# Shift taps of the convolution's keys: from diagonal matmuls to VectorE products in 16 bits

## The chip, the cores and the metric

The kernel runs on one core of a Trainium2 chip. The metric is the device time of one execution in microseconds (us). Engines: TensorE (PE; PEld is its weight load), VectorE (DVE), ScalarE (ACT), GpSimd (POOL) and the queue engine SyncE (SP), which here only issues transfers.

## The reference

Two independent blocks are computed and laid side by side in the output, A in columns 0 to 511, B in columns 512 to 1023.

```
A: qkv = x @ wqkv;  32 heads of width 16, 2048 rows
   p = softmax(q k^T / 4);  out_A = (p v) @ wo
B: k_shift[s] = sum over m = 0..3 of k[s - m] * shift_k[:, m]     (rows before 0 are zero)
   kv = k_shift * v
   y  = causal convolution of kv with ssm_k along the 2048 rows (by channel, 512 channels) + kv * ssm_D
   out_B = q * y
```

All inputs and the output are bfloat16.

## The kernel before

The Python program is a planner: it keeps a modelled clock for each engine (the class `Eng`, L181 on), decides step by step which work goes where, and writes out one fixed order of instructions per engine with the semaphore waits they need. Nothing is decided on the chip. A step T (the loop at the end of the kernel function) emits one set of score matmuls, one exponential on ScalarE, then values matmuls and whatever side work fits in the planned gap.

**Attention.** There are 2048 score blocks of 128 keys by 512 queries (32 groups n, each four heads by 512 queries, times 16 key tiles, times the four heads, one on each row group of TensorE). `emit_qk` (L896 within `qk_mm`) makes scores in PSUM banks 0 to 4. ScalarE takes two or three blocks at once (`emit_exp`, L921). Some blocks go another way (`dve_block` decides): VectorE turns the scores into 16-bit integers (`exp_on_dve`, L1010), GpSimd makes from them, by integer additions on 64-bit words, three shifted copies (`shift_ready`, L1030), and the four copies times four scaled sets of values make up the exponential. So such a block needs four values matmuls, one from ScalarE only one (`emit_pv`, L1122). Such blocks use PSUM bank 7 (`BGB`) or 5 (`DB`). The constants at the top of the file (LOW, R_LIN, LIN_D, T_DVE and others) say how many may be under way.

**Side work** also uses bank 7 and TensorE: projections of queries, keys and values (`pe_unit` and `evac_unit`, kinds q, k, v), the output projection (op), the convolution (`conv_lags`, L1372, 32 small matmuls for each of 128 groups of four channels), its turn back (L1399), and, before the change, the kind kv. Side units have due steps in the lists `early` and `jobs`, worked out from PLAN and constants such as K0, KS, K1, C2 and C3. Where the plan leaves TensorE idle, `warm_up` puts in small matmuls that add zero (L1577).

**The shifted keys before.** The keys are first copied to a scratch in DRAM with the two halves of the rows interleaved (`kt_scratch`, LKR rows). Three transposing loads (`load_kt`) bring them to SBUF with channels on partitions (`KTR`). GpSimd writes diagonal 128 by 128 matrices of the taps (`make_dg`, L690). A unit kv (there are 16: four slabs c of 128 channels, four quarters i of the rows) multiplies transposed keys with the four diagonals, so that turning back, shifting, scaling and summing happen in one accumulation in PSUM, 16 matmuls a unit:

```
for m in range(4):
    c0 = LEFT + 2 * (64 * (4 * i + 3 - b) - m)
    ins = e.matmul(PS[:, bank, 128 * b:128 * b + 128], lhsT=KTR[kt_i][:, kt_c, c0:c0 + 128], rhs=DG[:, c, m, :],
                   start=(m == 0), stop=(m == 3))
```

VectorE multiplies the result with the values `VST` (loaded by `load_v`, L632) and writes `KV`; `spread_kv` copies half of KV to other partitions by a transfer. Slabs 0 and 1 are done before step 60 or so (K0, K1), slabs 2 and 3 in the ranges of steps C2 and C3. The convolution of channels in a slab waits for it, and so do the turned results of later attention groups (`may_turn`), since they lie in the place of the diagonals.

**The filter.** `ssm_k` is loaded as it is (`KZN`), VectorE writes it in reverse order (`kz_turn`, four copies of 2048 elements, L675), adds the skip factor `ssm_D` at lag zero (`kz_store`) and stores it to a second scratch, from which the convolution's operands `WR` are loaded, two rows for each group of channels (`feed_wr`), 256 transfers in all.

**VectorE's order.** Urgent results (PSUM banks that others wait for) are placed by `urgent`; other pieces stand in the streams of `flow`, and `advance` puts them in where VectorE is free. `todo` adds up what is still pending there, and `dve_block` admits a further block only while that is small.

**Queues.** SP issues nearly all transfers, in program order: an entry that waits holds what stands behind it, among them the queries of the next pair of heads (`QT<-QS`, eight transfers of 16 KB each time). GpSimd's queue carries the output and the convolution's q.

Of the kernel before, what the change touches and what calls it, by code (L numbers as in the profile page):

```python
# [14 lines left out]
S = 2048  # L15
# [34 lines left out]
KT_LATE = 2.5  # L50
E1 = 17
ES = 1
NE = 4
K0 = 36
KS = 3
K1 = 46
E2 = 80
V2 = (20, 30)
V3 = (16, 49)
C2 = (95, 160)  # L60
C3 = (215, 280)
LOW_2 = 2
LOW_L = 2
LEAD = 2
PRESS = 0
YIELD = -4
# [3 lines left out]
HURRY = 2  # L70
LOW = 6
# [19 lines left out]
MOST_OP = 2  # L91
OVER_OP = 0.1
R_ARR = 8
R_LIN = 6
LIN_D = 1.0
EVEN = 0.85
MOST_D = 3
MORE = 0.1
ALONE = 0.3
T_DVE = 6  # L100
SLOT = 4
OPEN = 40
CLOSE = 0
S_U = 0.6
S_FX = 0.55
S_T = 0.2
S_C = 0.2
PLAN = 600
PACE = 580
# [3 lines left out]
LOOK = 10  # L113
SAFE = -1
PRIOR = 1
HOT = 20
MIN_L = 0
MIN_A = 2
# [4 lines left out]
OP0 = 26  # L123
EVEN_MORE = 6
MOST_L = 3
MANY = 2
DELAY = 1
SOON_P = 0.2
RATE = 0.38
LAST_P = 2.0  # L130
TAIL_GAP = 2
AHEAD = 5
KZ_LATE = 8.0
# [11 lines left out]
NEAR = 0.1  # L145
FULL = 1.0
# [4 lines left out]
V512 = (0.60, 0.726)  # L151
SHIFT = {1: (0.4, 0.55), 2: (0.615, 0.765), 4: (1.05, 1.2)}
# [21 lines left out]
    (0, {"DELAY": 1, "EVEN_MORE": 6, "FIRST": 1, "HALF": 0.35, "HURRY": 2, "JOIN": 0.15, "JOIN_D": 0.7, "LAGS": 12, "LATE": 0.3, "LATE_D": 0.3, "LEAD": 2, "LIN_D": 1.0, "LOW": 6, "LOW_2": 2, "LOW_A": 5, "LOW_L": 2, "MARGIN": 0.25, "MARGIN_D": 0.1, "MARGIN_P": 0.1, "MIN_L": 0, "NOW": 4, "OPEN": 40, "OVER_C": 0.1, "PRESS": 0, "PRIOR": 1, "R_LIN": 6, "SAFE": -1, "SOON": 0.3, "SOON_P": 0.2, "S_FX": 0.55, "TURN": 0.2}),  # L174
# [131 lines left out]
def bass_concat_heads__mha_block__ssm_conv_h3__prompt_kernel(  # L306
# [25 lines left out]
    def sb(name, shape, dt=BF16):  # L332
# [26 lines left out]
    SHK = sb("SHK", [128, 4, 4])  # L359
# [8 lines left out]
    VST = [x.rearrange("p (t d) -> p t d", t=NB)  # L368
           for x in (WR[:, R_W - 2, 0:S], WR[:, R_W - 1, 0:S], OUTA[:, :, :].rearrange("p r d -> p (r d)"), OUTA[:, :, :].rearrange("p r d -> p (r d)"))]
    KZS = WRF[:, 0:4 * LKZ].rearrange("p (c m) -> p c m", c=4)  # L370
    DSS = WRF[:, 4 * LKZ:4 * LKZ + 4].rearrange("p (c m) -> p c m", m=1)
    KTR = [QNF[:, 0:2 * LKR].rearrange("p (c s) -> p c s", c=2),
           OTF[:, 4 * QB:4 * QB + LKR].rearrange("p (c s) -> p c s", c=1),
           OTF[:, 4 * QB + LKR:4 * QB + 2 * LKR].rearrange("p (c s) -> p c s", c=1)]
    KT_OF = [(0, 0), (0, 1), (1, 0), (2, 0)]
    DG = OTF[:, 12 * QB + 2 * LEFT:16 * QB + 2 * LEFT].rearrange("p (c m d) -> p c m d", c=4, m=4)
    KZN = [OTF[:, 4 * QB:4 * QB + 2 * S].rearrange("p (c s) -> p c s", c=2),
           QNF[:, 0:2 * S].rearrange("p (c s) -> p c s", c=2)]
    XN = RST[:, R_ARR - 1, 0, :, :]
    PS = enter(nc.psum_tensor("PS", [128, 8, 512], FP32))  # L380
# [84 lines left out]
    h_shk = dma(sp, d_tap, SHK[:, :, :], B_shift_k.rearrange("(c p) m -> p c m", p=128), kb=4)  # L465
# [7 lines left out]
    h_vn, h_kt = [], {}  # L473

    def load_v(c, dep=None):
        for x in range(2):
            src = bass.AP(tensor=v2.tensor, offset=v2[S // 2 * x + 64 * (NB - 1), 128 * c].offset, ap=[[D, 64], [-64 * D, NB], [1, 128]])
            h = dma(sp, d_kv[3 + c], VST[c][x:128:2, :, :], src, [dep] if x == 0 else (), kb=256)
        h_vn.append(h)
    for c in range(3):  # L480
        load_v(c)
# [9 lines left out]
    def load_kt(i, dep):  # L491
        c0, c1 = ((0, 256), (256, 384), (384, 512))[i]
        h_kt[i] = dma(sp, d_kv[i], KTR[i][:, :, :], kt_ap[:, c0:c1], [dep, h_kpair[0]], transpose=True, kb=(1024, 512, 512)[i])
        done[(id(h_kt[i][0]), h_kt[i][1])] += KT_LATE

# [39 lines left out]
    def unit_deps(u):  # L535
        if u[0] == "q":
            return h_x[PAIRS[u[1]][1]] + [h_wq[min(PAIRS[u[1]][0], 1)]]
        if u[0] == "k":
            return h_x[u[2]] + [h_wk[min(u[1], 1)]]
        if u[0] == "kv":  # L540
            return [h_kt[KT_OF[u[1]][0]], h_dg[0]]
        return h_x[u[2]] + [h_wv[min(u[1], 1)]]

    def ready(u):
        if u[0] == "q":
            return (u[1] < R_Q or 2 * (u[1] - R_Q) + 1 in qk_done) and (u[1] < 2 or 2 * u[1] - 1 in h_q and at(h_q[2 * u[1] - 1]) <= pe.t + 0.5)
        if u[0] == "k":
            return u[1] < 2 or LAST[u[1] - 2] in qk_done
        if u[0] == "v":
            return u[1] < 2 or LAST[u[1] - 2] in pv_done  # L550
        if u[0] == "op":
            return (PAIRS.index((3, u[1])) if u[1] < NQB - 1 else (15, u[2] + 1)) in h_otn and h_wop[0] is not None
        return KT_OF[u[1]][0] in h_kt and (u[1] < 3 or len(h_vn) > 3 and at(h_vn[3]) <= pe.t)

    def pe_unit(u, bank, parts=(0, 1, 2, 3)):
# [19 lines left out]
        elif kind == "kv":  # L575
            _, c, i = u
            kt_i, kt_c = KT_OF[c]
            deps += [h_kt[kt_i], h_dg[0]]
            mm_run = 0.239

            def mm(e, b):
                ins = None
                for m in range(4):
                    c0 = LEFT + 2 * (64 * (4 * i + 3 - b) - m)
                    ins = e.matmul(PS[:, bank, 128 * b:128 * b + 128], lhsT=KTR[kt_i][:, kt_c, c0:c0 + 128], rhs=DG[:, c, m, :],  # L585
                                   start=(m == 0), stop=(m == 3))
                return ins
# [19 lines left out]
    def evac_unit(u, bank, h):  # L607
# [18 lines left out]
        elif kind == "kv":  # L626
            _, c, i = u
            u0 = NB - 4 - 4 * i
            val = VST[c][:, u0:u0 + 4, :].rearrange("p b (q g) -> p b q g", g=4)
            src = PS[:, bank, :].rearrange("p (b q g) -> p b q g", b=4, g=4)  # L630
            dst = KV[:, 32 * c:32 * c + 32, u0:u0 + 4, :].rearrange("p q w g -> p w q g")
            hh = urgent(lambda e: e.tensor_tensor(dst, src, val, ALU.mult), [h, h_vn[c]], us=V512)  # L632
            if kv_n[c] == 3:
                spread_kv(c, hh)
            kv_n[c] += 1
            if sum(kv_n[0:2]) == 8 and c < 2:
                load_qn(0, [h])
                open_wr(2, hh, True)
            if c >= 2 and kv_n[c] == 4:
                h_kvm[c - 2] = h  # L640
            if c == 2 and kv_n[c] == 4:
                load_v(3, hh)
# [9 lines left out]
    kv_n = [0] * 4  # L652
# [9 lines left out]
    wr_late = []  # L662
    h_kzw = [None]
    h_kzt = [None]
    h_dg = [None]
    early_dve = []
    flow.append(early_dve)

    def piece(make, deps, us=V512, gate=lambda: True):
        early_dve.append(("k", deps, make, us, gate))  # L670

    def kz_turn(c, us):
        rev = KZN[c // 2][:, c % 2, :]
        rev = bass.AP(tensor=rev.tensor, offset=KZN[c // 2][:, c % 2, S - 1:S].offset, ap=[rev.ap[0], [-1, S]])
        h_kzt[0] = dve.op(lambda e: e.tensor_copy(KZS[:, c, 0:S], rev), [h_kzl], us=us)  # L675
        if c == 3:
            load_kt(0, h_kzt[0])

    def kz_store(us):
# [5 lines left out]
        load_kt(1, h_kzt[0])  # L685
        load_kt(2, h_kzt[0])
        open_wr(R_W - 2, h_kzw[0])

    def make_dg(us):
        h_dg[0] = pool.op(lambda e: e.affine_select(  # L690
            out=DG, in_=SHK[:, :, :].rearrange("p c (m i) -> p c m i", i=1).broadcast_to([128, 4, 4, 128]),
            compare_op=ALU.is_equal, fill=0.0, base=0, pattern=[[0, 4], [0, 4], [-1, 128]], channel_multiplier=1),
            [h_shk], us=(3.0, 3.1))

    piece(make_dg, lambda: [], (0.0, 0.0))
    for c in (2, 3, 0, 1):
        piece(lambda us, c=c: kz_turn(c, us), lambda: [h_kzl], gate=lambda: dve.t >= at(h_kzl) + KZ_LATE)
    piece(kz_store, lambda: [h_kzt[0]], (0.1, 0.22))
# [146 lines left out]
    def todo():  # L845
        return max(dve.t - pe.t, 0.0) + sum(us[0] for f in flow for _, _, _, us, _ in f)
# [99 lines left out]
    def ends():  # L946
        return max(max(dve.t, pe.t) + sum(us[0] for f in flow for _, _, _, us, _ in f) + V512[0], pool.t + PAIR * len(shifts)) + PAIR + LAST_P

# [260 lines left out]
    def finish_group(n, j, h):  # L1209
# [25 lines left out]
        def may_turn():  # L1235
            return 2 * p in h_mul and 2 * p + 1 in h_mul and (p < 4 or kv_n[2] == 4) and (p < 8 or kv_n[3] == 4)
# [75 lines left out]
    def open_wr(k, dep, staged=False):  # L1312
        if wr_rows[0] == R_W - 2 and not staged:
            wr_late.append((k, dep))
            return
# [5 lines left out]
        if staged:  # L1321
            for late in wr_late:
                open_wr(*late)
# [97 lines left out]
    early += [(K0 + KS * i, ("kv", 0, i)) for i in range(4)] + [(K1 + KS * i, ("kv", 1, i)) for i in range(4)]  # L1421
# [7 lines left out]
    jobs += [(a + (b - a) * i // 3, ("kv", c + 2, i)) for c, a, b in ((0, *C2), (1, *C3)) for i in range(4)]  # L1429
# [25 lines left out]
    def unit_step(T):  # L1455
        tight = False
        while not tight:
# [21 lines left out]
            us = pe.turn("F") + (0.445 if u[0] == "turn" else 0.478 if u[0] in ("kv", "v") else 2 * MM) + SWITCH  # L1479
# [243 lines left out]
```

## Time and profile before

| | before |
|---|---|
| median of three runs | 703.47 us (703.36 to 703.57) |
| the profiled execution | 703.51 us |
| its span in the trace | 701.8 us |
| busy, ScalarE / TensorE | 675.3 / 676.3 us |
| busy, VectorE / GpSimd | 541.8 / 515.7 us |
| score blocks on VectorE | 585 of 2048 |
| bytes moved by DMA | 164.25 MB, mean 234 GB/s |

How to read the lines that follow. A busy share is an average over stages; an engine that idles is only of interest if something waits for it. A group's row gives line, engine, operation, output and inputs with their shapes, the count, then busy us and mean ns of one, then idle time of the engine just before and who ended it. In a row of waits stand the one that waits and the one waited for, then total us, number of times and the longest. In a row of stretches stand the bounds, the length, then busy us with counts of PE, PEld, DVE, ACT and POOL, the granted clock as a share of full speed, the busy share of the DMA engines and GB/s. A line of the timeline gives start and duration in us.

### The profile page before, as it was taken

Reading aid. Unit: us, or ns where it says so; the run is one execution under the profiler, and the core shown is the slowest. Engines: PE = TensorE matmul, PEld = TensorE weight load, DVE = VectorE, ACT = ScalarE, POOL = GpSimd, SP = SyncE. Lnnn points to the kernel's source line nnn. Section 1 sums busy time; section 2 is a strip of 40 time slices with the busy share of each in tenths; the row PEclk is TensorE's granted clock in tenths of the full one; section 3 lists DMA queues with packets and bytes.
Section 4 is the critical chain, followed back from the end, with each engine's and each line's share of the span. In section 5 each row is a group of like instructions: output and inputs, shape, how many; then the busy total and the mean of one; then the engine's idle time right before and its main releaser. Section 6 shows DMA issues by size and latency. Waiting matters only on the chain.

```text
span 701.8 us, 26112 instructions
## 1 busy us (share of the span) xinstructions
PE 676.3 (96%) x11426; PEld 274.0 (39%) x11426; DVE 541.8 (77%) x880; ACT 675.3 (96%) x654; POOL 515.7 (73%) x638
## 2 busy tenths in 40 slices
PE   9999999999999999999999999999999999999998
PEld 4334334444334443433434434343333434234354
DVE  5788788887887778777887778878778687777873
ACT  6999999999999999999989999999999999999986
POOL 5566788777677667777768889778778777788871
PEclk9999999999999999999999999999999999999999
DMA  9998672478766469687876777788686876668311
GB/s 228 267 279 258 145 252 89 170 277 270 257 245 203 162 244 321 197 279 242 337 278 205 220 256 257 280 311 327 221 320 230 316 280 233 223 218 311 75 46 33
DMA packets 83047, 164.25 MB, mean 234 GB/s; under 512 B 41232, under 2 KB 47256, under 8 KB 82680
## 3 DMA queue, kind: packets, MB, share of 16 engines
q1 hardware_dynamic: 79720, 155.58, 65.6%
q0 software_dynamic: 2016, 6.69, 3.7%
q8 instruction: 91, 1.49, 0.8%
q10 hardware_dynamic: 1200, 0.33, 0.2%
q14 instruction: 20, 0.16, 0.1%
HBM read 149.17 MB, written 8.54 MB: 225 GB/s over the span
## 4 chain that ended last, share of the span: by engine, by line
ACT 46%; PE 41%; DVE 8%; POOL 3%; issue 1%
ACT PT L921 46%; PE PS L1122 16%; PE PS L896 13%; PE PS L1372 3%; DVE RST L1010 3%; PE PS L1287 2%; POOL RST L1030 2%; PE PS L564 2%; PE PS L585 1%; PE PS L573 1%; PE PS L596 1%; DVE DTN L1224 1%; DVE DT L1213 1%; PE PS L1399 1%; POOL out_dram L401 1%
## 5 line engine op out<-in xcount | busy, mean ns | idle before, releaser
L921 ACT ACTIVATE PT<-PS 128x1024 bf16<-128x1024 f32 (+1 forms) x648 | 672.3, 1192 | 17.1 <-PE PS L896 15.8
L1030 POOL INT64_ADD RST<-RST x600 | 489.1, 818 | 161.4 <-DVE RST L1010 122.1
L1010 DVE TENSOR_SCALAR RST<-PS 128x512 uint16<-128x512 f32 x585 | 396.1, 687 | 123.1 <-PE PS L896 118.3
L1122 PE MATMUL PS<-PT,VA 128*32 128x512 bf16 (+2 forms) x1618 | 273.4, 365 | 1.4 <-POOL RST L1030 1.3
L896 PE MATMUL PS<-QT,KTo 32*128 32x512 bf16 (+2 forms) x2248 | 258.1, 364 | 15.2 <-ACT PT L921 4.2
L1122 PE MATMUL PS<-RST,VS 128*32 128x512 bf16 (+1 forms) x1890 | 265.1, 369 | 1.6 <-issue 1.1
L896 PEld LDWEIGHTS PS<-QT,KTo 32*128 32x128 bf16 x2248 | 67.7, 91 | 188.4 <-ACT PT L921 107.3
L1122 PE MATMUL PS<-RST,VA 128*32 128x512 bf16 (+1 forms) x630 | 132.5, 370 | 0.7 <-DVE DT L1213 0.3
L1372 PE MATMUL PS<-WR,KV 128*30 128x128 bf16 (+7 forms) x4096 | 106.2, 220 | 0.7 <-DVE VA L647 0.7
L1122 PEld LDWEIGHTS PS<-PT,VA 128*32 128x32 bf16 x1618 | 66.7, 94 | 73.8 <-issue 46.1
L1372 PEld LDWEIGHTS PS<-WR,KV 128*32 128x32 bf16 (+7 forms) x4096 | 80.3, 101 | 32.7 <-issue 7.0
L1122 PEld LDWEIGHTS PS<-RST,VS 128*32 128x32 bf16 x1890 | 64.7, 95 | 55.4 <-issue 31.0
L1122 PEld LDWEIGHTS PS<-RST,VA 128*32 128x32 bf16 x630 | 33.4, 94 | 20.4 <-issue 10.6
L1213 DVE STREAM_TRANSPOSE DT<-PS 128x512 f32<-128x512 f32 x31 | 22.1, 713 | 3.0 <-PE PS L1122 2.2
L1388 DVE CAST YB<-PS 128x512 bf16<-128x512 f32 x32 | 21.7, 679 | 0.0
L1224 DVE TENSOR_TENSOR DTN<-DT,DR 128x256 bf16<-128x256 f32 x31 | 19.6, 634 | 0.8
L1287 PE MATMUL PS<-WKV,OTN 128*128 128x512 bf16 (+1 forms) x68 | 19.6, 372 | 0.4 <-DVE OTN L1262 0.3
L596 PE MATMUL PS<-WKV,xT 128*128 128x128 bf16 x256 | 18.6, 220 | 0.2
L573 PE MATMUL PS<-xT,WKV 128*128 128x512 bf16 (+1 forms) x64 | 17.0, 376 | 0.8 <-DVE QS L612 0.8
L1577 PE MATMUL PS<-IDN,ZW 128*32 128x128 bf16 (+3 forms) x78 | 17.1, 287 | 0.0
L596 PEld LDWEIGHTS PS<-WKV,xT 128*128 128x128 bf16 x256 | 14.4, 98 | 7.1 <-issue 2.3
L564 PE MATMUL PS<-xT,WQ 128*128 128x512 bf16 x60 | 16.6, 383 | 0.1
(73 smaller groups left out, 215.3 us busy)
## 6 DMA issues: line engine op xcount, KB each, us to landing
WR<-kz_scratch SPq DMA_DIRECT2D x256, 528.0 KB, 6.1
kz_scratch<-WR SPq DMA_DIRECT2D x4, 544.0 KB, 4.6
kt_scratch<-in_B_k_dram SPq DMA_DIRECT2D x1, 2048.0 KB
QN<-in_B_q_dram POOLq DMA_DIRECT2D x4, 512.0 KB, 8.5
out_dram<-QN POOLq DMA_DIRECT2D x4, 512.0 KB, 8.8
QT<-QS SPq DMA_DIRECT2D x120, 16.0 KB, 3.7
out_dram<-OUTA POOLq DMA_DIRECT2D x15, 128.0 KB, 3.5
QN<-in_B_ssm_k_dram SPq DMA_DIRECT2D x1, 1024.0 KB, 9.0
```

The costliest lines, as they stand in the source:

```text
L564: return e.matmul(PS[:, bank, :], lhsT=WQ[:, dc, o * 128:(o + 1) * 128], rhs=xT[:, dc, qb * 512:(qb + 1) * 512], start=(dc == 0), stop=(dc ...
L573: return e.matmul(PS[:, bank, c0:512], lhsT=WK[:, dc, o * 128:(o + 1) * 128], rhs=xT[:, dc, sc * 512 + c0:(sc + 1) * 512], start=(dc == 0) ...
L596: ins = e.matmul(PS[:, bank, 128 * j:128 * j + 128], lhsT=xT[:, dc, (4 * sc + j) * 128:(4 * sc + j + 1) * 128], rhs=WV[:, dc, o * 128:(o + ...
L896: ins = e.matmul(PS[:, bank, i * w:i * w + w], lhsT=KTo[32 * s:32 * s + 32, OF[n_] % 2, kt * 128:(kt + 1) * 128], rhs=QT[32 * s:32 * s + 3 ...
L921: h_exp[T] = act.op(lambda e: e.activation(PT[:, p0:p0 + n, :].rearrange("p b f -> p (b f)"), PS[:, banks[0]:banks[0] + n, :].rearrange("p ...
L1010: st["h"].append(urgent(lambda e: e.tensor_scalar(lin[:, 0, half, :].bitcast(U16), PS[:, bank, :], FIX_ADD, FIX_HI, ALU.add, ALU.min), [h, ...
L1030: return pool.op(lambda e: e.int64_add(dst, src, by * WORDS), deps, us=SHIFT[k])
L1122: ins = e.matmul(dst, lhsT=w, rhs=rhs, start=first, stop=last, tile_position=(0, 32 * s))
L1213: h_t = urgent(lambda e: e.transpose(out=dt, in_=PS[:, PVB, :]), [h, h_mul.get(n - 1)], slack=S_T, us=(0.63, 0.751))
L1224: h_mul[n] = dve.op(lambda e: e.tensor_tensor(dtn.rearrange("p (b i) -> p b i", i=32)[:, :, DH * r:DH * r + DH], blocks[:, :, 0:DH], rcp.b ...
L1287: ins = e.matmul(PS[:, b, c0:c1], lhsT=OTN[:, PAIRS.index((o, qb)), t * 128:(t + 1) * 128], rhs=WO[:, o, c0:c1], start=(o == 0), stop=(o = ...
L1372: ins = e.matmul(dst, lhsT=KV[:, channel(qd) // 4, 2 * n:2 * NB, g], rhs=WR[:, (2 * qd + g // 2) % (R_W), w0:w0 + 128], start=(n == 0), st ...
```

## The change

The kind kv is gone from TensorE, with the diagonals and the transposing loads. Instead the keys stay with rows on partitions. There are eight batches j of 256 channels by four row tiles. For each, `load_kv` loads the keys four times from the scratch, each time shifted by one row more (four transfers of 256 KB with runs of 512 bytes), and the values (two transfers). The taps are loaded to all partitions (`load_shk`, twice, in place of a load of 4 KB), and GpSimd spreads them into a free part of `KV` (`scales`). VectorE then runs eight instructions on 1024 elements a partition (`products`): four scalings in place, three additions, and the product with the values into `KV`. Each waits for the one before. Batches 0 and 1 are loaded at the start, 2 and 3 when the reversal copies have freed their place, 4 to 7 one after the other from a planned time LATE_KV on. The reversal of the filter (`kz_turn`) goes to GpSimd. The planner leaves the products out of what `todo` counts, except for a flat 2 us (BACK) while one of the first four batches is ready. Some forty of its constants have other values.

```
-KT_LATE = 2.5
-E1 = 17
+LATE_KV = 90
+GAP_KV = 10
+KV_RATE = 180
+BACK = 2
+E1 = 21
...
-LOW = 6
+LOW = 8
...
-R_LIN = 6
-LIN_D = 1.0
+R_LIN = 7
+LIN_D = 1.5
...
-T_DVE = 6
+T_DVE = 4
...
-PLAN = 600
-PACE = 580
+PLAN = 540
+PACE = 560
...
 V512 = (0.60, 0.726)
+V1024 = (0.75, 0.88)
+POOL_COPY = (2.4, 2.5)
+POOL_SCALES = (1.6, 1.7)
...
+    def load_kv(j, deps):
+        c0, u0 = 256 * (j // 4), 4 * (j % 4)
+        d = d_kv[min(j, 3)]
+        for m in range(4):
+            r0 = LEFT + 128 * (NB - 1 - u0) - 2 * m
+            src = bass.AP(tensor=kt_ap.tensor, offset=kt_ap[r0:r0 + 1, c0:c0 + 1].offset, ap=[[D, 128], [-128 * D, 4], [1, 256]])
+            dma(sp, d, KST[min(j, 3)][:, m, :, :], src, [*deps, h_kpair[0]] if m == 0 else (), kb=256, rate=KV_RATE)
+        for x in range(2):
+            src = bass.AP(tensor=v2.tensor, offset=v2[S // 2 * x + 64 * (NB - 1 - u0), c0:c0 + 1].offset, ap=[[D, 64], [-64 * D, 4], [1, 256]])
+            h = dma(sp, d, VST[j if j < 4 else j % 2][x:128:2, :, :], src, kb=128, rate=KV_RATE)
+        return h
...
-        h_kzt[0] = dve.op(lambda e: e.tensor_copy(KZS[:, c, 0:S], rev), [h_kzl], us=us)
-        if c == 3:
-            load_kt(0, h_kzt[0])
+        h_kzt[0] = pool.op(lambda e: e.tensor_copy(KZS[:, c, 0:S], rev), [h_kzl], us=POOL_COPY)
+        if c == 0:
+            h_kv[2] = load_kv(2, [h_kzt[0]])
+        if c == 1:
+            h_kv[3] = load_kv(3, [h_kzt[0]])
...
+    def scales(i):
+        def make(us):
+            h_ws[i] = pool.op(lambda e: e.tensor_copy(WS[:, i, :, :, :], SHK), [h_shk if i == 0 else h_shk2[0]], us=POOL_SCALES)
+            if i == 0:
+                h_shk2.append(load_shk(1, [h_ws[0]]))
+        piece(make, lambda: [], (0.0, 0.0), lambda: pe.t >= at(h_shk if i == 0 else h_shk2[0]), early_pool)
...
+    def products(j):
+        i = j // 4
+        k, v, u0 = KST[min(j, 3)], VST[j if j < 4 else j % 2], 4 * (j % 4)
+        last = [None]
+
+        def step(fn):
+            def make(us):
+                last[0] = dve.op(fn, [last[0] if last[0] is not None else h_kv[j], h_ws[i]], us=us)
+            piece(make, lambda: [last[0] if last[0] is not None else h_kv[j], h_ws[i]], V1024, gate=lambda: j in h_kv and h_ws[i] is not None)
+
+        def scale(m):
+            x = k[:, m, :, :].rearrange("p t (r e) -> p t r e", e=64)
+            w = bass.AP(tensor=KV.tensor if hasattr(KV, "tensor") else KV, offset=WS[:, i, m, 0:1, 0:1].offset,
+                        ap=[KV[:, 0, 0, :].ap[0], [0, 4], [8 * NB, 4], [1, 64]])
+            step(lambda e: e.tensor_tensor(x, x, w, ALU.mult))
+
+        def add(m):
+            a, b = [k[:, x, :, :].rearrange("p t d -> p (t d)") for x in (3, m)]
+            step(lambda e: e.tensor_tensor(a, a, b, ALU.add))
+        scale(3)
+        for m in (2, 1, 0):
+            scale(m)
+            add(m)
+        dst = KV[:, 64 * i:64 * i + 64, u0:u0 + 4, :]
+        a, b = [x.rearrange("p t (q g) -> p q t g", g=4) for x in (k[:, 3, :, :], v[:, :, :])]
...
     def todo():
-        return max(dve.t - pe.t, 0.0) + sum(us[0] for f in flow for _, _, _, us, _ in f)
+        wait = BACK if early_dve and kv_n[0] < 4 and early_dve[0][4]() and at(*early_dve[0][1]()) <= pe.t else 0.0
+        return wait + max(dve.t - pe.t, 0.0) + sum(us[0] for f in flow if f is not early_dve for _, _, _, us, _ in f)
...
-    early += [(K0 + KS * i, ("kv", 0, i)) for i in range(4)] + [(K1 + KS * i, ("kv", 1, i)) for i in range(4)]
...
-    jobs += [(a + (b - a) * i // 3, ("kv", c + 2, i)) for c, a, b in ((0, *C2), (1, *C3)) for i in range(4)]
```

More of the change, by code (lines that the diff above doesn't have):

```diff
@@ new lines, in bass_concat_heads__mha_block__ssm_conv_h3__prompt_kernel, with make @@
+    h_kv = {j: load_kv(j, ()) for j in range(2)}
+    h_row = []
+    def products(j):
[20 more added lines that the diff above has]
+        a, b = [x.rearrange("p t (q g) -> p q t g", g=4) for x in (k[:, 3, :, :], v[:, :, :])]
+        def make(us):
+            h = dve.op(lambda e: e.tensor_tensor(dst, a, b, ALU.mult), [last[0]], us=us)
+            kv_n[0] += 1
+            if j % 4 == 3:
+                for c in (2 * i, 2 * i + 1):
+                    spread_kv(c, h)
+                h_kvm[i] = h
+            if j < 2:
+                (open_row if h_kzw[0] is not None else h_row.append)(h)
+            if j == 2:
+                load_qn(0, [h])
+            if 3 <= j < 7:
+                piece(lambda us: later(j + 1, h), lambda: [], (0.0, 0.0), gate=lambda: pe.t >= LATE_KV + GAP_KV * (j - 3))
+            if j < 3:
+                products(j + 1)
+        piece(make, lambda: [last[0]], V1024)
@@ L946, in ends @@
     def ends():
-        return max(max(dve.t, pe.t) + sum(us[0] for f in flow for _, _, _, us, _ in f) + V512[0], pool.t + PAIR * len(shifts)) + PAIR + LAST_P
+        return max(max(dve.t, pe.t) + sum(us[0] for f in flow if f is not early_dve for _, _, _, us, _ in f) + V512[0], pool.t + PAIR * len(shifts)) + PAIR + LAST_P
     def dve_block(T, n_act, aside, chosen):
```

171 lines of the change are left out of this document (61 added, 110 removed).

## The prediction

> **What bounds the kernel now.** I read the page first: busy time by engine, then the chain that ended last.
>
> ```profile
> PE 676.3 (96%) x11426; PEld 274.0 (39%) x11426; DVE 541.8 (77%) x880; ACT 675.3 (96%) x654; POOL 515.7 (73%) x638
> ...
> ACT 46%; PE 41%; DVE 8%; POOL 3%; issue 1%
> ```
>
> Two engines are full at once, ScalarE (the exponentials) and TensorE, and the chain changes between them. Next the waits, longest first; the columns are total us, times, longest.
>
> ```profile
> POOL RST L1030 <- DVE RST L1010: 122.1, 146, 3.6
> DVE RST L1010 <- PE PS L896: 118.3, 317, 2.1
> PEld PS L896 <- ACT PT L921: 107.3, 274, 0.9
> ...
> PEld PS L1122 <- POOL RST L1030: 39.2, 154, 0.8
> ...
> ACT PT L921 <- PE PS L896: 15.8, 41, 1.6
> ```
>
> It is a ring. GpSimd waits for VectorE, VectorE for scores from TensorE, the score matmuls for a bank that ScalarE frees, and ScalarE hardly at all. So time falls only when ScalarE gets fewer of the 2048 score blocks, that is when VectorE and GpSimd take more of them by the shift road. The groups give the price of a block on each road, and a piece of the chain gives what values matmuls cost.
>
> ```profile
> L921 ACT ACTIVATE PT<-PS 128x1024 bf16<-128x1024 f32 (+1 forms) x648 | 672.3, 1192 | 17.1 <-PE PS L896 15.8
> L1030 POOL INT64_ADD RST<-RST x600 | 489.1, 818 | 161.4 <-DVE RST L1010 122.1
> L1010 DVE TENSOR_SCALAR RST<-PS 128x512 uint16<-128x512 f32 x585 | 396.1, 687 | 123.1 <-PE PS L896 118.3
> ...
> L1577 PE MATMUL PS<-IDN,ZW 128*32 128x128 bf16 (+3 forms) x78 | 17.1, 287 | 0.0
> ```
>
> ```profile
> 123.99 0.76 PE PS L1122 x12
> ```
>
> 585 blocks went to VectorE, so ScalarE had 1463: 672.3 / 1463 = 0.46 us each. A block on the other road costs VectorE 396.1 / 585 = 0.677 us and GpSimd 489.1 / 585 = 0.836 us, and it needs four values matmuls in place of one. Twelve of these took 0.76 us, so three more cost TensorE 0.19 us, and up to 0.25 us more (four matmuls) if its scores need a turn of their own.
>
> Last, three stretches of the run (length, then busy us of PE, PEld, DVE, ACT, POOL):
>
> ```profile
> 80.00:110.00 30.00, 29.00 (x430) 10.46 (x430) 25.53 (x41) 28.95 (x31) 23.03 (x29) 1.00 0.70 208
> 110.00:170.00 60.00, 59.23 (x1024) 24.72 (x1021) 48.48 (x77) 59.42 (x60) 45.87 (x56) 1.00 0.62 213
> ...
> 300.00:600.00 300.00, 291.17 (x5184) 114.80 (x5183) 237.29 (x373) 295.13 (x289) 233.01 (x286) 1.00 0.77 270
> ```
>
> VectorE held 79% over the long middle (237.29 / 300), 81% from 110 to 170 and 85% from 80 to 110 us. This is the share the forecast turns on.
>
> **The change, part by part.** What goes:
>
> ```profile
> sum 701.00, PE 18.63 PEld 14.35; mean PE 1.43 PEld 1.10
> ```
>
> ```profile
> L632 DVE TENSOR_TENSOR KV<-PS,WR 128x512 bf16<-128x512 f32 x8 | 5.5, 686 | 3.4 <-PE PS L585 3.4
> L632 DVE TENSOR_TENSOR KV<-PS,OUTA 128x512 bf16<-128x512 f32 x8 | 5.5, 684 | 0.9 <-PE PS L585 0.9
> ...
> L690 POOL TENSOR_SCALAR_AFFINE_SELECT OTN<-SHK 128x2048 bf16<-128x2048 bf16 x1 | 2.0, 2019 | 6.6 <-DMA SHK<-in_B_shift_k_dram 6.6
> ...
> L675 DVE COPY WR<-QN 128x2048 bf16<-128x2048 bf16 x2 | 1.5, 784 | 0.0
> ...
> L675 DVE COPY WR<-OTN 128x2048 bf16<-128x2048 bf16 x2 | 1.3, 632 | 0.0
> ```
>
> The first row is the sum of the stretches of line 585 alone, the diagonal matmuls: TensorE loses 18.6 us. VectorE loses the 16 products from PSUM (5.5 + 5.5) and the four reversals (1.5 + 1.3), 13.8 us. GpSimd loses the 2.0 us that made the diagonals. The bank of the side units also comes free 16 times.
>
> What comes: eight batches of eight VectorE instructions (four scalings, three additions, the product with the values), 64 in all, each with 1024 elements a partition, 16-bit, both inputs in SBUF. The trace has no such instruction. The nearest with two SBUF inputs are these (ns min/median/max):
>
> ```profile
> L1224 DVE TENSOR_TENSOR DTN<-DT,DR x31: 407/666/1079, 40.6 to 674.6; 128x256 bf16<-128x256 f32 x31
> ...
> L1257 DVE TENSOR_TENSOR DTN<-DT,DR x4: 224/445/765, 681.1 to 697.9; 128x64 bf16<-128x64 f32 x4
> ```
>
> ```profile
> L1224 DVE TENSOR_TENSOR DTN<-DT,DR 128x256 bf16<-128x256 f32 x31 | 19.6, 634 | 0.8
> ```
>
> Upper end: from 64 to 256 elements the shortest grew by 183 ns, 0.95 ns an element; 1024 would take 407 + 768 x 0.95 = 1.14 us, and with the mean excess of line 1224 over its shortest, 634 - 407 = 0.227 us, 1.37 us. Lower end: the 2048-element copy with one input took 0.632 us, half of it is 0.32 us. I take the 0.75 us that the diff writes down for this shape (V1024). It lies between, and its neighbour V512, 0.60 us, stands in the code against 0.677 us a block measured, so such figures are near what runs here. 64 x 0.75 = 48.0 us; net VectorE +34.2 us, to 576.0 us or 82.1% of the present span.
>
> GpSimd gets four reversals and two spreads of the taps. The nearest row is the 2.02 us of the diagonals (same 2048 elements); the code writes 2.4 and 1.6. I take the code's: 9.6 + 3.2 - 2.0 = +10.8 us, inside GpSimd's 161 us of idling. Bounds: 8 us (2.02 each for four) to 16 us (twice the row each). If that cover were gone it would delay shifts and so values matmuls, which now wait 39.2 us for GpSimd.
>
> The loads: keys come back from scratch four times (8 x 4 x 256 KB) in place of three transposes, and the taps as 2 x 256 KB.
>
> ```profile
> 0.00:60.00 60.00, 56.16 (x589) 22.67 (x589) 42.52 (x88) 53.31 (x50) 35.51 (x47) 1.00 0.98 259
> ```
>
> ```profile
> 14.58 10.51 SPq L401 DMA_DIRECT2D WR<-in_B_v_dram x4
> 25.12 2.08 SPq L401 DMA_DIRECT2D OUTA<-in_B_v_dram x2
> 27.25 4.54 SPq L401 DMA_DIRECT2D kt_scratch<-in_B_k_dram x2
> 31.83 0.65 SPq L401 DMA_DIRECT2D kt_scratch<-ZW x1
> 32.53 5.05 SPq L401 DMA_DIRECT2D QT<-QS x8
> ```
>
> The DMA engines are full for the first 60 us (share 0.98, 259 GB/s). Up to the first half of the products, before moved 2.0 (scratch) + 2.0 (transposes) + 1.5 MB (values), after moves 2.0 + 0.5 + 4 x 1.25 MB: 2 MB more, 8 us at that rate. On SP's queue the first two batches' 12 transfers wait for the scratch rows, and the QT<-QS of the second pair of heads stand behind them. I cost this at nothing, because the convolution is the only reader and its matmuls are spread over the whole run; the price if wrong is the 8 us. The third and fourth batches wait in SP's queue for GpSimd's reversals; behind them stand the filter rows, which need those reversals anyhow, and the later QT<-QS. Batches five to eight wait for the product before them, late enough that nothing but WR feeds stands behind.
>
> **The sum.** Were only TensorE and ScalarE to count, d blocks would move until both had gained the same: 18.6 - 0.19 d = 0.46 d gives d = 28.6 and 13.1 us (9.5 us at 0.44 us per block). That is the ceiling, 690.4 us. VectorE takes part of it: at a share s, 576.0 + 0.677 d = s (701.8 - 0.46 d). s = 0.84, a little under its best stretch: d = 12.7, a gain of 5.9 us. s = 0.821: nothing. s = 0.80: d = -14, 6.4 us lost. I choose 0.84 because the products may run whenever VectorE idles (they are not counted by the planner when it decides on further blocks) and 16 turns of the side bank are free. The profiled execution took 703.51 us around a span of 701.8, equal to the median 703.47 within 0.04, so 703.5 - 5.9 = 697.6, said as 698.
>
> **A rule that speaks against it.** Two instructions of line 1224 and GpSimd's beside them:
>
> ```profile
> 59.84 0.79 DVE L1224 TENSOR_TENSOR DTN<-DT,DR 128x256 bf16<-128x256 f32 x1
> ```
>
> ```profile
> 59.74 1.79 POOL L1030 INT64_ADD RST<-RST  x2 [0.26 <-DVE RST L1010]
> ```
>
> ```profile
> 40.60 0.41 DVE L1224 TENSOR_TENSOR DTN<-DT,DR 128x256 bf16<-128x256 f32 x1
> ```
>
> Started 0.10 us after a GpSimd pair, the product took 0.79 us; begun with GpSimd idle, 0.41. The Trainium skill, SBUF — State Buffer, section "SBUF: two separate sides", says that a VectorE instruction with two SBUF inputs and a GpSimd one that reads SBUF exclude each other for a whole instruction; the trace agrees with 0.79 against 0.41. The skill's VectorE: DVE Perf Modes, section on the perf-mode tiers, gives 1224 ns for a 2048-element 16-bit product, so an estimate of 0.69 us for ours, before such a wait; with it the sum would be 0.69 + 0.23 = 0.92 us each, near no change.
>
> **The rivals.**
> Lock: the 0.227 us comes on top of 0.75. 64 x 0.98 = 62.5 us, VectorE 590.5, at s = 0.84 d = -0.9: 703.9 us; at the upper end of 1.37 us, d = -25 and 715. Against it: 0.75 may hold the wait already. It decides from a mean of 0.97 us on.
> VectorE as the bound (the other side): VectorE cannot rise above some 80%, since it waits for scores in a fixed order; then d = -14 and 710 us; at today's 77%, 719. For it: 79% over 300 us with 118 us of waits that are not its own. It decides at a share of 82.1%.
> Early loads: the second pair's queries come late by the 8 us, ScalarE idles: 697.6 + 8 = 706 us. For it: share 0.98.
> Nothing: the freed TensorE time turns into more of line 1577's fillers (17.1 us now) and the count of blocks stays: 703.5 us. For it: fillers exist today, so TensorE's time is not short everywhere. Against it: it is full to 97% over the middle 300 us, and 16 turns of the side bank come free with it.
>
> **How the numbers follow.** Forecast 0.50; VectorE bound 0.17; lock 0.16, a quarter of it within 0.2%; early loads 0.08; nothing 0.05; others 0.04, spread on both sides. 0.2% (1.4 us) is about what a measurement can tell from no change. Faster 0.53, same 0.08, slower 0.39. The range leaves out the ceiling's last us and the far ends of the lock and of VectorE at 77%: 690 to 714. The forecast's own range is 690 to 702.
>
> **What would show it.** Line 585's group gone, 64 instructions near 0.75 us on VectorE; its share 83 to 85%; line 1010 at about 598 instead of 585 and ScalarE's busy time 6 us lower. Wrong if the count of line 1010 falls, if the new instructions take 1 us or more, or if ScalarE's waits in the first 80 us grow by several us.

## The result and the profile after

The changed kernel takes 714.81 us against 703.52 us: ratio 1.0162, 95% interval 1.0135 to 1.0188. The prediction was 698 us; the sign is wrong, and the time lies 0.8 us above the range's upper end. The profiled execution took 714.70 us around a span of 712.7 us, before 703.51 around 701.8, so 10.9 us of span are to be found. The page of the changed kernel, busy time and the chain that ended last:

```profile
PE 670.5 (94%) x11208; PEld 263.4 (37%) x11208; DVE 572.8 (80%) x922; ACT 679.4 (95%) x657; POOL 540.4 (76%) x645
...
ACT 41%; PE 32%; DVE 17%; POOL 6%; DMA 3%; issue 1%; SPq 1%
```

VectorE's part of the chain grew from 8 to 17%. The groups that answer to those shown before (line 949 is ScalarE's exponential, 1038 a block on VectorE, 1058 the shifts, 1597 the fillers):

```profile
L949 ACT ACTIVATE PT<-PS 128x1024 bf16<-128x1024 f32 (+1 forms) x651 | 676.5, 1172 | 24.5 <-PE PS L924 22.9
L1058 POOL INT64_ADD RST<-RST x602 | 505.4, 843 | 155.8 <-DVE RST L1038 121.0
L1038 DVE TENSOR_SCALAR RST<-PS 128x512 uint16<-128x512 f32 x583 | 391.0, 685 | 107.0 <-PE PS L924 101.8
...
L1597 PE MATMUL PS<-IDN,ZW 128*32 128x256 bf16 (+3 forms) x122 | 28.9, 290 | 0.8 <-DVE QS L600 0.4
```

VectorE took 583 blocks, not 598 (585 before). The 18.6 us of diagonal matmuls are gone, but TensorE's busy time fell by only 5.8: fillers rose from 17.1 to 28.9 us. Its waits for VectorE rose as well, before (first) and after (second):

```profile
PEld PS L896 <- DVE RST L1010: 24.9, 67, 1.1
...
PE PS L896 <- DVE RST L1010: 2.3, 9, 0.6
```

```profile
PEld PS L924 <- DVE RST L1038: 37.4, 84, 1.7
...
ACT PT L949 <- PE PS L924: 22.9, 53, 3.7
PE PS L924 <- DVE RST L1038: 10.5, 29, 1.2
...
PEld PS L1394 <- DMA WR<-kz_scratch: 3.9, 1, 3.9
PE PS L1394 <- DMA WR<-kz_scratch: 3.6, 1, 3.6
```

The tap instructions, by shape (the largest group, of 20, and the two extremes of the scalings):

```profile
L685 DVE TENSOR_TENSOR OTN<-OTN,KV 128x1024 bf16<-128x1024 bf16 x20 | 18.5, 923 | 0.0
...
L685 DVE TENSOR_TENSOR WR<-WR,KV 128x1024 bf16<-128x1024 bf16 x8 | 8.5, 1066 | 0.0
...
L685 DVE TENSOR_TENSOR QN<-QN,KV 128x1024 bf16<-128x1024 bf16 x4 | 2.9, 722 | 0.0
```

All 64 sum to 56.6 us, 0.885 each. Consecutive instructions overlap at their ends, so the added time on the engine is less: from the start of one to the start of the next, idle time left out, 0.82 us in the mean, 52.3 us in all, against the 0.75 that the planner used and the prediction took.

**Where the time went.** The trace gives the moment at which the N-th of the 2048 score blocks was finished (ends of lines 949 and 1038, counted):

| N | 100 | 200 | 300 | 600 | 700 | 1200 | 1300 | 2000 |
|---|---|---|---|---|---|---|---|---|
| before, us | 47.1 | 81.5 | 114.4 | 213.6 | 246.0 | 413.9 | 444.9 | 676.4 |
| after, us | 47.8 | 81.5 | 116.2 | 218.9 | 253.1 | 418.5 | 456.7 | 687.4 |
| lag, us | 0.7 | 0.0 | 1.8 | 5.3 | 7.1 | 4.6 | 11.8 | 11.0 |

There are two places. The first lies between 81 and 253 us (7 us, of which 2.5 are made up later), the second near 435 us (7 us at once). The stretches of both kernels, before first (the columns are those of the prediction: bounds, length, busy us of PE, PEld, DVE, ACT, POOL, granted clock, DMA share, GB/s):

```profile
42.00:95.00 53.00, 50.78 (x683) 20.09 (x678) 40.21 (x63) 50.76 (x48) 38.43 (x47) 1.00 0.82 225
95.00:240.00 145.00, 141.82 (x2373) 56.88 (x2370) 116.81 (x184) 143.40 (x143) 107.50 (x133) 1.00 0.62 211
```

```profile
42.00:95.00 53.00, 45.66 (x491) 14.87 (x495) 51.80 (x80) 51.12 (x45) 46.79 (x44) 1.00 0.66 211
95.00:240.00 145.00, 134.29 (x2131) 50.28 (x2123) 133.20 (x206) 140.23 (x136) 113.15 (x126) 1.00 0.69 219
...
430.00:435.00 5.00, 3.13 (x71) 1.28 (x67) 2.24 (x4) 4.03 (x4) 4.18 (x5) 1.00 1.02 257
435.00:440.00 5.00, 3.29 (x51) 0.94 (x51) 1.82 (x3) 2.27 (x3) 1.38 (x2) 0.75 1.03 420
440.00:445.00 5.00, 5.00 (x65) 1.60 (x64) 2.00 (x4) 3.10 (x4) 3.38 (x5) 0.56 1.02 414
445.00:450.00 5.00, 5.00 (x96) 1.95 (x93) 4.46 (x8) 5.00 (x7) 3.72 (x6) 1.00 0.64 202
```

From 42 to 95 us VectorE is busy for 51.80 of 53 us (98%; before 76%), from 95 to 240 us 92% (before 81%), and TensorE falls from 98 to 93% there. Near 435 us the granted clock falls to 0.75 and 0.56. TensorE's timeline after (start, length, then what was issued; the idle time before it in brackets) shows why:

```profile
436.71 0.65 PE L1394 MATMUL PS<-WR,KV 128*32 128x128 bf16 x32 [3.58 <-DMA WR<-kz_scratch]
437.29 0.83 PE L924 MATMUL PS<-QT,KTo 32*128 32x512 bf16 x6
```

A convolution step waited 3.58 us for its filter rows. SP's and GpSimd's timelines tell what held the rows:

```profile
412.64 9.63 SPq L401 DMA_DIRECT2D QT<-QS  x8
```

```profile
421.75 2.18 POOL L401 DMA_DIRECT2D QN<-in_B_q_dram  x2
```

SP's queue stood behind the queries of the next heads until 422.3 us, half a microsecond after GpSimd had begun to issue two loads of the convolution's q, 512 KB each. The view of the DMA issues (count, KB each, median us to landing), before from 395 to 420 us and after from 420 to 445 us:

```profile
WR<-kz_scratch SPq DMA_DIRECT2D x9, 528.0 KB, 5.1
QN<-in_B_q_dram POOLq DMA_DIRECT2D x2, 512.0 KB, 6.8
```

```profile
WR<-kz_scratch SPq DMA_DIRECT2D x11, 528.0 KB, 13.1
QN<-in_B_q_dram POOLq DMA_DIRECT2D x2, 512.0 KB, 10.6
```

Before, q was issued at 396.6 us and had landed by 405.2 us, and the next rows were issued from 402.7 us on, so the two hardly met. The wait, and the lower clock behind it, stand at the second loss; how much of it they make is for the runs below. The Trainium skill, TensorE: Matmul & The Clock Gate, Part 1, says that at least one idle window of about 3.4 us halves the clock, and that at least one busy window of that length brings it back; the trace agrees with 3.58 us of idling before the granted 0.75 and 0.56. If the clock was half, these two shares come to 2.5 and 4.4 us of it (an estimate), and it was back at 1.00 only about 8 us after work had begun again at 436.7 us.

### The profile page after: what moved, and what is told of

Read it like the earlier page. It is cut to its first block, busy times and chain, and to the rows that moved or that the text cites. A ratio compares the mean times of both kernels' runs of the same rounds, so it can differ in the third digit from the quotient of the medians.

```text
span 712.7 us, 25755 instructions
## 1 busy us (share of the span) xinstructions
PE 670.5 (94%) x11208; PEld 263.4 (37%) x11208; DVE 572.8 (80%) x922; ACT 679.4 (95%) x657; POOL 540.4 (76%) x645
## 4 chain that ended last, share of the span: by engine, by line
ACT 41%; PE 32%; DVE 17%; POOL 6%; DMA 3%; issue 1%; SPq 1%
ACT PT L949 41%; PE PS L1150 12%; PE PS L924 10%; DVE RST L1038 8%; POOL RST L1058 5%; PE PS L1394 3%; PE PS L1315 2%; DMA WR<-kz_scratch 2%; DVE OTN L685 2%; PE PS L574 1%; DVE OTN L689 1%; DVE DTN L1252 1%; PE PS L584 1%; PE PS L565 1%; DMA xT<-in_A_x_dram 1%
## 5 line engine op out<-in xcount | busy, mean ns | idle before, releaser
L1058 POOL INT64_ADD RST<-RST x602 | 505.4, 843 | 155.8 <-DVE RST L1038 121.0
L1038 DVE TENSOR_SCALAR RST<-PS 128x512 uint16<-128x512 f32 x583 | 391.0, 685 | 107.0 <-PE PS L924 101.8
L1150 PE MATMUL PS<-PT,VA 128*32 128x512 bf16 (+2 forms) x1620 | 279.4, 367 | 3.3 <-POOL RST L1058 2.8
L1150 PE MATMUL PS<-RST,VA 128*32 128x512 bf16 (+1 forms) x628 | 128.8, 371 | 2.2 <-POOL RST L1058 1.7
L1394 PE MATMUL PS<-WR,KV 128*32 128x128 bf16 (+7 forms) x4096 | 107.2, 221 | 3.6 <-DMA WR<-kz_scratch 3.6
L1150 PEld LDWEIGHTS PS<-PT,VA 128*32 128x32 bf16 x1620 | 69.8, 94 | 79.3 <-issue 49.2
L1394 PEld LDWEIGHTS PS<-WR,KV 128*24 128x24 bf16 (+7 forms) x4096 | 80.9, 101 | 36.7 <-issue 8.4
L1597 PE MATMUL PS<-IDN,ZW 128*32 128x256 bf16 (+3 forms) x122 | 28.9, 290 | 0.8 <-DVE QS L600 0.4
L685 DVE TENSOR_TENSOR OTN<-OTN,KV 128x1024 bf16<-128x1024 bf16 x20 | 18.5, 923 | 0.0
```

Source lines behind the costliest of these rows:

```text
L685: step(lambda e: e.tensor_tensor(x, x, w, ALU.mult))
L1038: st["h"].append(urgent(lambda e: e.tensor_scalar(lin[:, 0, half, :].bitcast(U16), PS[:, bank, :], FIX_ADD, FIX_HI, ALU.add, ALU.min), [h, ...
L1058: return pool.op(lambda e: e.int64_add(dst, src, by * WORDS), deps, us=SHIFT[k])
L1150: ins = e.matmul(dst, lhsT=w, rhs=rhs, start=first, stop=last, tile_position=(0, 32 * s))
L1394: ins = e.matmul(dst, lhsT=KV[:, channel(qd) // 4, 2 * n:2 * NB, g], rhs=WR[:, (2 * qd + g // 2) % (R_W), w0:w0 + 128], start=(n == 0), st ...
L1597: pe.op(lambda e, s=s, dst=dst, rhs=rhs, rows=rows, first=first: e.matmul(dst, lhsT=ZW[:, 0:rows], rhs=rhs, start=first, stop=first, tile_ ...
```

## The experiments

The first question was whether the first loss comes from the lock, GpSimd's adds being held up by tap instructions that read two tiles from SBUF (theory A), or is VectorE's own time (theory B); the letters are those of the expectations. For A speaks that adds that overlap a tap instruction took 1.07 us in the mean against 0.81 for the others, and that the chain of the changed kernel runs over GpSimd's adds and a GpSimd copy alone from 46.4 to 75.0 us; against it, block 200 comes at 81.5 us in both kernels. The second question was whether the filter row is the whole of the second loss.

**Taps replaced by fills, same order.**

```
-step(lambda e: e.tensor_tensor(x, x, w, ALU.mult))
+step(lambda e: e.memset(k[:, m, :, :].rearrange("p t d -> p (t d)")[:, 0:608], 1.0))
-step(lambda e: e.tensor_tensor(a, a, b, ALU.add))
+step(lambda e: e.memset(k[:, 3, :, :].rearrange("p t d -> p (t d)")[:, 0:608], 1.0))
```

> The 56 scalings and additions on VectorE are replaced by fills of 608 elements with a constant (near 0.68 us each, what the shortest scalings took, and no input in SBUF); the convolution's keys are thus not computed. The order of all instructions stays that of the changed kernel. Theory A (instructions with two SBUF inputs and GpSimd's additions shut each other out): GpSimd's 602 additions fall from 843 ns to about 815 ns, no GpSimd-bound stretch from 46 to 76 us, and some 7 us of the 10.9 us that the changed kernel lost go, about 708 us. Theory B (it is VectorE's time as such that is missing): the 64 instructions still take some 45 us, so at most 2 us are won, 713 us or more. Theory C (a late filter row at 433 us and the clock after it) is not touched: the wait of 3.6 us on that row and the lower clock are still there in both.

Measured: 707.97 us, ratio 1.0052 (1.0037 to 1.0068). The lag at block 700 is gone (246.3 us, before 246.0), and at block 1200 the kernel is 2.8 us ahead of before; then it loses the filter row's wait (5.2 us here). But the fill was shorter than the product that it was meant to equal:

```profile
L685 DVE MEMSET OTN<- 128x608 bf16 x20 | 11.3, 565 | 1.5
```

0.565 us, where a tap instruction without an add beside it takes 0.62 to 0.68. So it took away both causes at once, and A and B stayed apart no further than before.

**Taps kept with two SBUF inputs, but on 8 elements.**

```
-step(lambda e: e.tensor_tensor(x, x, w, ALU.mult))
+x8, w8 = k[:, m, 0, 0:8], WS[:, i, m, 0, 0:8]
+step(lambda e: e.tensor_tensor(x8, x8, w8, ALU.mult))
-step(lambda e: e.tensor_tensor(a, a, b, ALU.add))
+a8, b8 = a[:, 0:8], b[:, 0:8]
+step(lambda e: e.tensor_tensor(a8, a8, b8, ALU.add))
```

> The same 56 instructions keep their two SBUF inputs, their place and their waits, but work on 8 elements a partition in place of 1024 (the keys are not computed). Theory A: each still waits for a running GpSimd addition, but holds GpSimd up hardly at all; time near that of the fills, 707 us. Theory B: VectorE's busy time falls by some 40 us and now the loss goes, 707 us, while the fills stay at 713 us. So the two differ only in the fills, and this run says how much of the loss hangs on these instructions at all: if it stays above 712 us, neither A nor B is the cause.

Measured: 708.59 us, 1.0053 (1.0034 to 1.0073), block 700 at 245.9 us. Short instructions with the lock lose as little as short fills without it; again both A and B can say that (the lock is held for a shorter time).

**Second q load cut to 8 of 64 rows.**

```
-h_qn[i] = dma(pool, d_q[0], QN[64 * x:64 * x + 64, :, :], ...)
+n = 64 if i == 0 else 8
+h_qn[i] = dma(pool, d_q[0], QN[64 * x:64 * x + n, :, :], ...[0:n])
```

> The second load of q for the convolution's output (issued on GpSimd's queue at 421.8 us, 1 MB) moves 8 of each 64 rows, an eighth; the output of the second half of the convolution is not valid. Order unchanged. Theory C1 (this load delays the filter rows): the wait of 3.6 us at 433 us falls under 1 us, the clock stays at 1.00, about 709 us. Theory C2 (the rows were issued late, behind the transfers of the queries on SP's queue, and the DMA load does not matter): the wait stays near 3 us, 714 us.

Measured: 710.66 us, 1.0085 (1.0056 to 1.0113). The wait for the row is gone, and with it the drop of the clock, as the stretch from 430 to 450 us shows, after (first) and here (second):

```profile
430.00:450.00 20.00, 16.42 (x275) 5.77 (x272) 10.52 (x17) 14.39 (x16) 12.65 (x16) 0.83 0.93 323
```

```profile
430.00:450.00 20.00, 17.62 (x310) 6.57 (x307) 14.48 (x23) 17.86 (x19) 15.81 (x20) 1.00 0.86 316
```

The lag at block 700 stays (252.9 us). Between blocks 1200 and 1300 the lag now grows by 3.0 us in place of 7.1. So the meeting of q and the rows makes most of the second loss; what makes the other 3 us at this place stays open.

**Both: short fills and the small q load.**

> The fills of 608 elements in place of the 56 scalings and additions and the small second load of q together, order unchanged. If the two causes add up: e1 stood at 450.4 us at its 1300th block with a wait of 5.2 us on a filter row behind it; without that wait, and with the clock at 1.00, some 7 us less than e1, 700 to 702 us, which would account for the whole loss of the changed kernel. If the stall comes from the queue's order as well, or another wait takes its place, 705 us or more.

Measured: 704.00 us, 0.9999 (0.9972 to 1.0026), between the two expected ranges; block 700 at 245.7, block 2000 at 675.6 us. Against the kernel before of the same call the loss was 11.3 us in the changed kernel, 4.2 with the fills, 6.9 with the small q and 0.5 with both: the fills take away 7.1, the small load 4.4, the two 10.8. Within the two or three microseconds by which such differences are uncertain, the two causes add up to the whole loss.

**Both, with fills of 996 elements** (`[:, 0:608]` becomes `[:, 0:996]`, the small q load stays): a fill as long as the mean tap instruction, that reads nothing.

> As the run with fills and the small load of q together (ratio 0.9999 to before), but each of the 56 fills writes 996 elements in place of 608, so that it takes VectorE some 0.89 us, as long as the scalings and additions took with their waits (the keys are again not computed, the second half of q only in part). Theory A (what costs is that GpSimd is shut out): no change against the shorter fills, 702 to 705 us, GpSimd's additions near 814 ns. Theory B (VectorE's time itself): 18 us more on VectorE than with 608 elements bring the loss back, 708 to 711 us.

Measured: 714.94 us, 1.0140 (1.0113 to 1.0166), above even the 708 to 711 us expected for theory B. Adds, fills, and the waits of TensorE:

```profile
L1058 POOL INT64_ADD RST<-RST x602 | 488.0, 813 | 175.8 <-DVE RST L1038 140.2 <-DVE DR L1282 0.9 <-PE PS L1150 0.4
...
L685 DVE MEMSET OTN<- 128x996 bf16 x20 | 17.8, 888 | 3.1 <-DVE RST L1038 1.6 <-issue 1.3 <-DVE DTN L1252 0.2
```

```profile
PEld PS L924 <- DVE RST L1038: 39.0, 84, 1.8
PEld PS L1150 <- POOL RST L1058: 32.6, 128, 1.0
...
PE PS L924 <- DVE RST L1038: 15.1, 39, 1.3
```

GpSimd's adds are back at 813 ns (after: 843, before: 818) and its results are waited for less than before (32.6 against 39.2 us), yet the loss is there and larger, block 700 at 257.8 us, and TensorE's waits for VectorE are the changed kernel's and more. The run before it differs in the length of the fills alone and has its adds at 814 ns. That settles it for B: VectorE's time is enough to cost this much, with no add held up. It also gives a price. Added time on VectorE (start to start of all 64 instructions, plus the idle time before them) and loss, filter row out of the way:

| | added VectorE time, us | loss against before, us |
|---|---|---|
| short fills | 33.9 + 4.5 = 38.4 | 0.5 |
| the real taps | 52.3 | 6.9 |
| long fills | 51.8 + 9.0 = 60.8 | 10.7 |

A little under half a microsecond of time for each further microsecond of VectorE, from three points that are each uncertain by about 2 us, in an order written for shorter instructions.

The lock is not cleared by this, for it works on VectorE too. In the changed kernel 37 of the 64 tap instructions started while a GpSimd add was running. 35 of them ended 0.54 to 0.56 us after that add did, however long it still ran, and the 37 took 0.99 us in the mean; the other 27 took 0.68 in the median. That is about 37 x 0.31 = 11.5 us more on VectorE, and by the table's slope some 5 of the 6.9 us lost. This is an estimate: no run has full taps without the lock.

**The filter's reversal at half its length** (with the small q load; the copy moves 1024 32-bit words and doesn't reverse).

```
-h_kzt[0] = pool.op(lambda e: e.tensor_copy(KZS[:, c, 0:S], rev), [h_kzl], us=POOL_COPY)
+h_kzt[0] = pool.op(lambda e: e.tensor_copy(KZS[:, c, 0:S].bitcast(U32), KZN[c // 2][:, c % 2, :].bitcast(U32)), [h_kzl], us=POOL_COPY)
```

> As the run with the small second load of q (710.7 us), but the four filter copies on GpSimd move 1024 words of 32 bits in place of 2048 of 16 bits, and not in reverse order (the filter is thus wrong); order unchanged. If GpSimd's 8 us of reversals in the first 48 us are part of the loss, half of them gives 2 us or more back, 708.5 us or less; if the early stretch has cover, within 1 us of 710.7 us.

Measured: 710.44 us, 1.0075 (1.0052 to 1.0099), against 710.66 with the small q load alone. The copies took 1.03 to 1.14 us in place of 2.0 to 2.2. The reversal on GpSimd is hidden, to within the 1 us by which the lag at block 700 shrank (5.9 us, with the small q load alone 6.9).

**Q later by the plan**: `at(h_out[0]) < pe.t - 1.0` becomes `- 12.0`, with the order written anew from about 420 us on.

> The changed kernel whole, only the second load of q is issued some 8 us later by the plan (a margin of 12 in place of 1 us behind the first half's output); the plan changes from about 420 us on. Theory C1 (the load of q collides with the filter rows): no long wait on a filter row, clock 1.00, as with the small load, 707 to 711 us. If the collision only moves, one wait of over 2 us on a filter row elsewhere and 713 us or more.

Measured: 713.20 us, 1.0122 (1.0084 to 1.0160). The wait for the filter row shrank to 1.0 us and the clock stayed at 1.00, but VectorE now waited 3.1 us for q, and the lag grew from 6.8 us at block 1300 to 8.6 at block 2000. Moving the load moved the wait.

**TensorE's relief alone**: the kernel before with one diagonal matmul in place of four, and the plan told so.

```
-mm_run = 0.239
+mm_run = 0.06
-for m in range(4):
+for m in range(1):
-us = pe.turn("F") + (0.445 if u[0] == "turn" else 0.478 if u[0] in ("kv", "v") else 2 * MM) + SWITCH
+us = pe.turn("F") + (0.445 if u[0] == "turn" else 0.12 if u[0] == "kv" else 0.478 if u[0] == "v" else 2 * MM) + SWITCH
```

> The kernel before with one diagonal matmul in place of four in each kv unit (three of four taps are left out, so the convolution's keys are not the reference's); the planner is told that such a unit is short, all constants stay. TensorE so loses three quarters of the 18.6 us, and VectorE and GpSimd pay nothing. Theory D (my sum: freed TensorE time turns into blocks for VectorE): 18.6 x 0.75 = 14 us freed, three quarters of the ceiling of 13.1 us, some 694 us and 20 blocks more on VectorE. Theory E (the count of blocks is set by banks, queues and the planner's conditions, and freed time ends in fillers): count within 5 of 585, 701 to 705 us.

Measured: 701.03 us, 0.9958 (0.9930 to 0.9986).

```profile
L1010 DVE TENSOR_SCALAR RST<-PS 128x512 uint16<-128x512 f32 x585 | 393.9, 687 | 120.4 <-PE PS L896 116.1
...
L1577 PE MATMUL PS<-IDN,ZW 128*32 128x512 bf16 (+3 forms) x82 | 19.9, 288 | 0.6 <-DVE DT L1213 0.6
```

Three quarters of the diagonal matmuls gone for nothing in return bring 2.4 us and not one block more. **The same with the constants chosen anew** (some 40 of them, LOW_A, JOIN_D, K0, PACE and the like):

> The kernel with one of four taps on TensorE (three taps left out) and constants chosen anew for it; its order puts 598 blocks on VectorE. Theory D with a fitting order: 13 blocks x 0.46 = 6 us of ScalarE less than before, 694 to 698 us. Theory E holds in the strict form (freed TensorE time is worth nothing) if it is above 700 us.

Measured: 701.73 us, 0.9971 (0.9952 to 0.9991). Now VectorE has 598 blocks, and the gain is no larger: ScalarE waits 17.8 us for scores (12.4 without the new constants) and TensorE 3.4 us for filter rows. At block 1000 this order is 3.4 us ahead of before and at block 1200, with the longest of these waits between, 1.1; what it would gain without them is open.

**Is it the constants that came with the change?** The changed kernel with the constants that both kernels have (28 of them, PLAN, PACE, T_DVE, R_LIN and others) put back to the values before:

> The changed kernel with the 28 constants that both have set back to the values of before; the products, the loads and the reversal on GpSimd stay. The order puts 579 blocks on VectorE (585 before, 583 changed). Theory A (lock) and E (count of blocks): 6 blocks fewer cost ScalarE 6 x 0.46 = 2.8 us and the lock some 7 us, 711 to 714 us without a stall. If the loss of the changed kernel came from its other constants, this one is below 707 us.

Measured: 716.94 us, 1.0175 (1.0133 to 1.0217), above the 711 to 714 us expected. Putting them back does not bring the time back. This order loses in part elsewhere: it lags 5.9 us at block 700, 8.3 at block 2000 and 13.6 at the last.

**A plan that knows of the longer instruction**: 0.60 us for a tap instruction, 0.25 more and 0.5 on GpSimd's clock where GpSimd is busy, and constants chosen for it.

```
-V1024 = (0.75, 0.88)
+V1024 = (0.60, 0.73)
+held = pool.t > dve.t
+last[0] = dve.op(fn, ..., us=(us[0] + 0.25, us[1] + 0.25) if held else us)
+if held:
+    pool.t += 0.5
```

> The changed kernel with a planner that knows of the exclusion: a product that finds GpSimd busy is planned 0.25 us longer, and GpSimd 0.5 us later; its constants are chosen anew for that. 578 blocks on VectorE. Theory A: the cost of the lock stays (GpSimd's additions near 840 ns) but no longer pushes TensorE's order out of step, so some 4 to 8 us of the 10.9 us come back, 703 to 708 us. If 712 us or more, foresight does not help.

Measured: 709.22 us, 1.0059 (1.0033 to 1.0085), 5.3 us over before in place of 11.3 and just above the 703 to 708 expected. It has no wait for a filter row, and the lag at block 700 is 9.2 us, larger than in the changed kernel; at block 1200 it is 5.1 and at block 2000 4.9 us. What it gains on the changed kernel it gains at the second place; foresight of the length did not mend the first loss.

None of the runs of the full computation beats the kernel before. Whether another placing of the taps could is open. Holding SP's order alone fixed, and full taps without the lock, were not tried.

## Why the prediction was wrong

**The step that failed is the choice of the share in the sum, s = 0.84 and with it d = +12.7.** The blocks went to d = -2 and VectorE's share to 80.4% (572.8 / 712.7). Of the reasons given for 0.84, that the products may run whenever VectorE idles is the one the traces refute: the products land between 42 and 240 us, where VectorE was at 76 and 81% and went to 98 and 92%. An average over 700 us hid how little idle time there was where the work came: 41 us (198 less 40.2 and 116.8), of which the change used 28, and the score blocks no longer got their turn in time. The equation had a second fault: it gave all time to ScalarE's blocks. With the measured share of 0.804 it gives d = -11, and -2 was measured. ScalarE has two blocks more and its idle time grew from 26.5 to 33.3 us, because scores came late behind VectorE.

**TensorE's 18.6 us** were sized rightly and the diagonals are gone, but they bought nothing: 11.8 us became fillers, and the waits for VectorE rose by 12.5 us at the weight loads and 8.2 at the matmuls. The ceiling of 13.1 us falls as well. With three quarters of the relief for free the chip gave 2.4 us, and 13 more blocks gave no more. That the ring turns TensorE's time into blocks at 0.46 us each was argued from waits and did not show in either run.

**The price of a tap instruction**, 0.75 us: 0.885 us as the trace has it, 0.82 from start to start, so 52.3 us in place of 48.0. Without an add or a copy running on GpSimd as it starts it takes 0.62 to 0.68 us, with an add 0.92 in the median. The estimate of 0.69 + 0.23 = 0.92 us in the prediction, from the Trainium skill's VectorE: DVE Perf Modes, section on the perf-mode tiers, came nearest to the mean. Put into the prediction's own formula, 52.3 us would have moved the point of no change to a share of 82.7% and the gain from 5.9 to 4.0 us, so by that formula this term explains 1.9 of the 17 us by which the forecast is off.

**The rivals.** VectorE as the bound is the nearest: 710 us at s = 0.80, against 710.7 with the filter row taken out. Its mechanism held, by the stretches and the long fills; its sum did not, since it had d = -14 where the count hardly moved and the time was lost in waits, so that the two numbers agree is luck. Its chance of 0.17 was too small: the row that spoke for it, 79% over 300 us with waits that were not its own, was quoted, and the choice went by the best stretch instead. The lock is real (0.2 us on each instruction in the mean) and stayed below the 0.97 us from which it decides by the prediction (0.96 by its own formula). But that mark prices VectorE's time in blocks alone; at the price measured in the runs with fills, the lock is by estimate some 5 us of the loss. Early loads: block 200 comes at 81.5 us in both kernels; the extra 2 MB were hidden, as costed. Nothing: its mechanism, more fillers and the same count, came true, its time not.

**GpSimd** was right: the reversals and spreads took 10.9 us where 12.8 was costed, and half the reversal's time changes 0.2 us by the medians.

**What no step named** is the second place, 4.4 us of the time by the run with the small q load. The prediction followed SP's queue at the start, and not what a new order does to a load of 1 MB on GpSimd's queue 400 us later.

## What to carry to other kernels

Where the order is written out beforehand, work moved to another engine has to fit the idle time of the stretch where it lands; look up the share there, not over the run. Time freed on one engine of a ring is worth what the next engine can take, and a run that frees it for nothing tells that before anything is built. An instruction that has to wait out one of a neighbour engine costs its own engine that wait: here 0.99 us in place of 0.68. After a new order, look for the one transfer that now meets another: a single wait of 3.6 us, with the lower clock behind it, cost 4.4 us.

## What was not expected of the hardware

A VectorE fill of 608 16-bit elements took 565 ns and of 996 elements 888 ns, 0.83 ns an element, with about 0.16 us of idle time before each long one (9.0 us before 56), where the tap products had none. A 16-bit product of 1024 elements from SBUF, 0.62 us at its shortest, took up to 2.26 us: that one began at 42.82 us beside a reversing copy on GpSimd and ended 0.54 us after the copy, as those begun beside an add did. A GpSimd copy of 2048 16-bit elements in reverse took 2.0 to 2.2 us. From 440 to 445 us a TensorE that never idled was granted 0.56 of its clock in the mean, and its matmuls of 512 columns took 0.61 us against 0.39 before the wait.
